# Phase 2 with seven block products instead of eight

## The chip, the cores and the metric

The kernel runs on one core of one Trainium2 chip. The metric is the device time of one execution in microseconds (us). A core has a matmul engine (PE, TensorE; PEld are its weight loads), three engines for elementwise work (DVE, ACT and POOL), and a queue engine (SP) from which this kernel issues its DMAs. Each engine works through its own instructions in the order in which the program puts them; semaphores tie the engines together.

## What is computed

Three layers one after the other, all in float32 (condensed from the reference):

```python
def _attn_ref(q, k, v):                  # 4 batches, 8 heads, 576 positions, 64 wide
    scores = scale * np.matmul(q, k.transpose(0, 1, 3, 2))
    mask = (rel >= 0) & (rel < window)   # causal window of 128, linear bias per head
    attn = softmax(np.where(mask, scores + bias[None], -1000000000.0))
    return np.matmul(attn, v)
def _moe_ref(x, w1, w2, w3, w_out):      # x: 2304 x 512, d_ff 1024
    h = (x @ w1) * (x @ w2) @ w3
    return h @ w_out
def _moe2_ref(x, w_in, w_out):           # d_ff 2048
    h = np.maximum(x @ w_in, 0.0)
    return h * h @ w_out
```

The attention output, 2304 tokens of 512, goes through the first feed-forward layer (called g and y below) and then through the second. Only the second, "phase 2", is computed differently by the change: r = max(x w_in, 0), then o = (r * r) w_out. Weights arrive as 64-bit floats and are made into float32 words on the chip.

## The kernel before

**Precision.** Every float32 operand of a matmul that counts is split into a high part and the rest, each in the format that PE reads at full rate (F32R). A product is then three matmuls, high x high, high x low and low x high, which `mm3` (lines 163 to 166) issues. So each operand costs a copy (the high part) and a subtraction (the low part) on DVE, ACT or POOL before PE can use it.

**Phase 1** holds attention for 32 heads, the first layer's two products and their product (`add_ab`, names `g`, `gf`, `gt`), and the second (`add_y`), which stores y transposed to DRAM, `y_scr`. Its order is made by a planner (`Plan`, lines 28 to 121): each piece of work is a task with a rank, the engines that could do it with an assumed length on each, what it depends on, and the buffers that it takes and gives back. The planner places tasks one by one, the earliest first and the lower rank among those that could start at about the same time, chooses the engine where more than one can do it, and so fixes each engine's order. [...]

**Weights.** A 64-bit word is turned into a float32 word by a scaling (`conv_g`), a shift (`conv_s`) and two shift-and-mask instructions (`conv_m`, line 294) on 1024 columns; `conv_hi` and `conv_lo` split the result. Phase 2's weights are 16 such pieces, `w2io`: piece fi holds 128 columns of w_in and the 128 rows of w_out that belong to them. Six are converted in phase 1 by the planner, ten within the first 512 tokens of phase 2 by a fixed order.

**Phase 2** (`r_step`, `o_step`, lines 934 to 990) is written out by hand. Tokens go in four blocks of 512 and one of 256. For each block and each fi, `r_step` multiplies 128 columns of w_in with the block's y (four inner pieces of 128, three matmuls each, 512 columns wide), ACT takes Relu and Square, and DVE splits the square into `rr`. Two steps later `o_step` multiplies `rr` with the rows of w_out and adds to the block's accumulators in PSUM, one for each 128 tokens (512 columns wide), over all 16 fi. The squares stay in SBUF.

## Time and profile before

| | us |
|---|---|
| median of 3 runs (lowest, highest) | 921.34 (920.14, 923.11) |
| the profiled execution | 921.4 |
| its span, first to last instruction | 919.6 |
| phase 1, to the first r matmul | 515.9 |
| phase 2, first r matmul to the last matmul's end | 399.9 |

The profile's page gives busy times by engine, and a chain that follows the work that ended last back to the start. Rows by line read: line, engine, operation, output<-input by tile names, partitions x elements, how many, then busy time, mean length in nanoseconds, and the idle time before them with what ended it. Rows of stretches read: from:to, length, then the busy time of PE, PEld, DVE, ACT and POOL with counts, the granted clock of PE (1.00 is full), the share of the DMA engines' time and GB/s. Rows of the timeline read: start, length, engine, line, operation; a matmul's length overlaps with the next one's, so the distance between starts is what a matmul costs. POOL's durations are rough.

### The profile page before, as it was taken

To read this page: it belongs to the slowest core of one execution; us is meant where nothing else is said; L and a number is where in the kernel's file an instruction comes from. 1 tells how busy PE (TensorE), PEld (TensorE's weight loads), DVE (VectorE), ACT (ScalarE), POOL (GpSimd) and SP (SyncE) were. 2 spreads that over 40 slices of the span, in tenths; PEclk is the share of its full clock that TensorE was granted. 3 is DMA by queue.
4 is the path that set the end of the run, shared out by engine and by line. 5 is a ranking of instruction groups with operands and counts; after the bars stand their busy time and mean duration, and the time that the engine had idled before them with its cause. 6 is when DMAs were issued, how large, how long until landed. Compare 5 with 4: busy or idle time off the path is not lost.

```text
span 919.6 us, 13785 instructions
## 1 busy us (share of the span) xinstructions
PE 908.6 (99%) x5192; PEld 777.8 (85%) x5192; DVE 515.7 (56%) x1189; ACT 417.5 (45%) x941; POOL 115.7 (13%) x166
## 2 busy tenths in 40 slices
PE   8999999999999999999999999999999999999998
PEld 5544479999999999999999888888888888888897
DVE  5777888787777777786749992132222112221222
ACT  5777776676666666663512442232223222222222
POOL 3323323142312122120000000000000000000000
PEclk9999999999999999999999999999999999999999
DMA  6786321423223132312626430020001000100010
GB/s 234 261 292 196 138 78 33 109 49 83 72 72 85 33 91 66 84 40 70 208 73 229 163 127 12 0 92 1 1 11 69 1 1 12 46 1 1 10 38 24
DMA packets 31075, 73.73 MB, mean 80 GB/s; under 512 B 5793, under 2 KB 14497, under 8 KB 26913
## 3 DMA queue, kind: packets, MB, share of 16 engines
q1 hardware_dynamic: 31008, 72.86, 25.6%
q8 instruction: 41, 0.67, 0.3%
q14 instruction: 26, 0.20, 0.1%
HBM read 63.41 MB, written 9.44 MB: 79 GB/s over the span
## 4 chain that ended last, share of the span: by engine, by line
PE 92%; DVE 4%; issue 1%; DMA 1%; ACT 1%; POOL 0%; SPq 0%; DVEq 0%; POOLq 0%; ACTq 0%
PE g L164 9%; PE g L166 9%; PE g L165 9%; PE o L165 7%; PE o L166 7%; PE o L164 7%; PE r L165 7%; PE r L166 7%; PE r L164 7%; PE g L725 7%; PE s L458 3%; PE t L481 2%; PE a L515 2%; PE s L461 1%; PE s L460 1%; DVE raw L294 1%
## 5 line engine op out<-in xcount | busy, mean ns | idle before, releaser
L947 DVE CAST rr<-s 128x512 fp32r<-128x512 f32 (+1 forms) x80 | 31.9, 399 | 250.0 <-ACT s L946 249.9
L945 ACT ACTIVATE t<-r 128x512 f32<-128x512 f32 (+1 forms) x80 | 44.4, 555 | 264.0 <-PE r L166 264.0
L164 PE MATMUL g<-x,wu 128*128 128x288 f32 x512 | 153.7, 300 | 0.0
L165 PE MATMUL g<-x,wu 128*128 128x288 f32 x512 | 151.5, 296 | 0.0
L166 PE MATMUL g<-x,wu 128*128 128x288 f32 x512 | 151.0, 295 | 0.0
L165 PE MATMUL r<-ys,wu 128*128 128x512 f32 (+1 forms) x320 | 118.8, 371 | 0.0
L166 PE MATMUL r<-ys,wu 128*128 128x512 f32 (+1 forms) x320 | 118.7, 371 | 0.0
L164 PE MATMUL r<-ys,wu 128*128 128x512 f32 (+1 forms) x320 | 118.6, 371 | 0.0
L165 PE MATMUL o<-wu,rr 128*128 128x512 f32 x288 | 113.2, 393 | 0.0
L166 PE MATMUL o<-wu,rr 128*128 128x512 f32 x288 | 112.7, 391 | 0.5 <-DVE rr L172 0.5
L164 PE MATMUL o<-wu,rr 128*128 128x512 f32 x288 | 112.8, 392 | 0.0
L165 PEld LDWEIGHTS g<-x,wu 128*128 128x128 f32 x512 | 96.9, 189 | 0.0
L166 PEld LDWEIGHTS g<-x,wu 128*128 128x128 f32 x512 | 96.5, 189 | 0.0
L164 PEld LDWEIGHTS g<-x,wu 128*128 128x128 f32 x512 | 96.4, 188 | 0.0
L294 DVE SCALAR_TENSOR_TENSOR raw<-raw 128x1024 uint32<-128x1024 uint32 x72 | 91.7, 1277 | 2.3 <-ACT raw L284 1.4
L165 PE MATMUL g<-gt,wu 128*128 128x288 f32 x256 | 75.8, 296 | 0.6 <-DVE gt L172 0.6
L164 PE MATMUL g<-gt,wu 128*128 128x288 f32 x256 | 76.3, 298 | 0.0
L166 PE MATMUL g<-gt,wu 128*128 128x288 f32 x256 | 75.5, 295 | 0.0
L164 PEld LDWEIGHTS r<-ys,wu 128*128 128x128 f32 x320 | 60.2, 188 | 11.7
L165 PEld LDWEIGHTS r<-ys,wu 128*128 128x128 f32 x320 | 60.2, 188 | 11.5
L166 PEld LDWEIGHTS r<-ys,wu 128*128 128x128 f32 x320 | 60.1, 188 | 11.0
L438 ACT ACTIVATE e<-e,st 128x256 f32<-128x256 f32 (+1 forms) x128 | 60.5, 475 | 17.0 <-DVE st L430 16.7
(123 smaller groups left out, 1662.5 us busy)
## 6 DMA issues: line engine op xcount, KB each, us to landing
raw<-in_w2io_dram SPq DMA_DIRECT2D x16, 1024.0 KB, 4.9
qkraw<-in_qk_dram SPq DMA_DIRECT2D x46, 288.0 KB, 4.3
raw<-in_w3t_dram SPq DMA_DIRECT2D x8, 1024.0 KB, 5.5
raw<-in_w_dram SPq DMA_DIRECT2D x8, 1024.0 KB, 5.1
y_scr<-ye SPq DMA_DIRECT2D x32, 144.0 KB, 1.8
out_dram<-ob SPq DMA_DIRECT2D x18, 256.0 KB, 2.4
raw<-in_w_out_dram SPq DMA_DIRECT2D x4, 1024.0 KB, 7.0
yr<-y_scr SPq DMA_DIRECT2D x16, 256.0 KB, 2.7
```

The lines of the kernel that those rows point to most:

```text
L164: nc.tensor.matmul(o, wh, xh, start=start, stop=False)
L165: nc.tensor.matmul(o, wh, xl, start=False, stop=False)
L166: nc.tensor.matmul(o, wl, xh, start=False, stop=stop)
L294: nc.vector.scalar_tensor_tensor(out=low, in0=high, scalar=(3, 0x80000000)[part], in1=low, op0=(ALU.logical_shift_left, ALU.bitwise_and)[p ...
L438: nc.scalar.activation(out=e, in_=e, func=ACTF.Exp, bias=st[:, 0, i:i + 1], scale=-1.0, accum_out=st[:, 1, i:i + 1],)
L458: nc.tensor.matmul(o, qb, d["kh"][:, k0:k1], start=True, stop=True)
L460: nc.tensor.matmul(o, qb, d["kh"][:, k0:k1], start=True, stop=False)
L481: nc.tensor.transpose(t[:, 128 * c:128 * c + 128], src, ident)
L515: nc.tensor.matmul(a[:, 128 * kb:128 * kb + w], vs[:, kb, :], pt[:, 0, c:c + w], start=kb == 0, stop=kb == 2,)
L725: nc.tensor.matmul(gw[fi], wl, wr, start=c == 0, stop=c == 7)
L945: nc.scalar.activation(out=t, in_=o, func=ACTF.Relu)
L947: nc.vector.tensor_copy(out=rr[:, 0, 0:n], in_=s)
```

## The change

Both products of phase 2 are computed by Strassen's scheme in Winograd's form: the matrices are cut into 2 x 2 blocks, sums of blocks are formed first, seven block products are taken instead of eight, and further sums give the four blocks of the result.

**r.** The three token ranges of 768 are passes j = 0, 1, 2. In a pass, w_in's 2048 columns are cut into halves (a row of the one belongs to one of the other 1024 away; m counts 8 pieces of 128 in a half), the inner 512 into halves of 256 and the tokens into halves of 384. A group (j, m) has seven products P1 to P7 into PSUM banks `X` (five), each of two inner pieces x three matmuls of 384 columns (`p_r`). Then `add_group` forms the sums: c1 (a copy of P1, on ACT), U2, U3 and U4 and the four results `C` (four buffers), seven DVE instructions that read PSUM. ACT takes Relu and Square of each C, and it is stored to DRAM, `s_scr`. All of r is done before o begins.

**o.** Nine groups t of 256 tokens. The squares are read back (four tiles of 128 partitions x 8 x 128, in runs of 512 bytes), four combinations of 1024 columns are formed (`fc0` to `fc3`), seven operands are split (`oh`, `ol`, 1024 columns, tiles `ww` and `st`), and each of the seven products has 8 inner pieces x three matmuls of 256 columns (`p_o`). Sums as above, then stores to the output.

**Weights.** All 16 conversions are now planner tasks of rank 500 and up behind the first layer's weights, inside phase 1; the words go to DRAM (`m_scr`). Piece m is read back when it is needed, combined (four sums of 256 columns, `cb`) and split into seven blocks: tile `u` for four of them (1024 columns) and `v6` or `u` for three (768). The ten `u` and six `v6` tiles hold all of w_in's blocks until the last pass of r lets go of them one after the other, and only then take w_out's.

**Order.** Phase 2 is in the planner now, with PE's products in a fixed sequence and all other work placed around them. Tile pools are opened at the points where the memory of the stage before is free: `fo` after pass 1 of r, `fq` and `ww` after the last product of r and the last o weights.

The diff, cut to its core:

```diff
+    TN = 384
+    NJ = NT // (2 * TN)
+    NM = NF2 // 2
+    s_scr = [dram.tile([NF2, 128, 2 * TN], F32, name=f"s_scr{j}") for j in range(NJ)]
+    m_scr = {(k, m): dram.tile([128, 1024], F32, name=f"m_scr{k}{m}") for k in "io" for m in range(NM)}
-            pt1=1, pt2=1, a=1, b=1, xf=1, ta=1, tb=1, g=3, asb=2, gf=2, gt=8, ye=2, w2v=4, yr=2,
+            pt1=1, pt2=1, a=1, b=1, xf=1, ta=1, tb=1, g=3, asb=2, gf=2, gt=8, ye=2,
+            yA=14, yB=6, s0=1, t2a=1, t2b=1, v6=6, st=2, c1=2, U2=1, U4=1, U3=1, C=4, X=5, fo=4, fq=5, ww=4,
...
-    def r_step(j, fi):
-        n = blocks[j][1]
...
-        for k in range(K1):
-            mm3(o, w[:, 0, k * 128:(k + 1) * 128], w[:, 1, k * 128:(k + 1) * 128],
-                y[:, 0, k, 0:n], y[:, 1, k, 0:n], k == 0, k == K1 - 1)
...
-        nc.scalar.activation(out=t, in_=o, func=ACTF.Relu)
-        nc.scalar.activation(out=s, in_=t, func=ACTF.Square)
-        nc.vector.tensor_copy(out=rr[:, 0, 0:n], in_=s)
-        sub(nc.vector, rr[:, 1, 0:n], s, f(rr[:, 0, 0:n]))
-        rt[j, fi] = rr
...
-        for i in range(nt):
-            mm3(acc[j][i], rr[:, 0, i * 128:(i + 1) * 128], rr[:, 1, i * 128:(i + 1) * 128],
-                w[:, 0], w[:, 1], fi == 0, fi == NF2 - 1)
-    LAG = 2
-    steps = [(j, fi) for j in range(NB) for fi in range(NF2)]
...
+    A_AT = {1: "a0", 2: "a1", 3: "b2", 4: "a3", 5: "b0", 6: "b1", 7: "a2"}
+    B_AT = {1: "a0", 2: "a2", 3: "a3", 4: "b2", 5: "b0", 6: "b1", 7: "a1"}
+    PO = (1, 6, 7, 5, 2, 3, 4)
+    ORDER = ((1, 2, 4, 6, 7, 5, 3), PO)
...
+    def open_q1():
+        att.close()
+        psb.close()
+        q = q1.enter_context(tc.tile_pool(name="q1", bufs=1, side="right", reuse_waits="tile"))
+        pool.update(yA=q, s0=q, t2a=q)
+        ps = late.enter_context(tc.tile_pool(name="ps_x", bufs=1, space=PSUM, reuse_waits="tile"))
+        pool.update(X=ps)
...
+    def open_fo():
+        yst.close()
+        pool["fo"] = yst.enter_context(tc.tile_pool(name="fo", bufs=1, reuse_waits="tile"))
+
+    def open_q2():
+        q1.close()
+        q = q1.enter_context(tc.tile_pool(name="q2", bufs=1, side="right", reuse_waits="tile"))
+        pool.update(fq=q, ww=q)
...
+    def m_last(k, m):
+
+        r = raws[k, m]
+        nc.vector.scalar_tensor_tensor(
+            out=flat(r), in0=r[:, :, 1], scalar=0x80000000, in1=r[:, :, 0],
+            op0=ALU.bitwise_and, op1=ALU.bitwise_or,
+        )
+
+    def m_store(k, m):
+        nc.sync.dma_start(out=m_scr[k, m], in_=f(flat(raws.pop((k, m)))))
...
+    def combine(kind, i, M, S, e):
+
+        if kind == "A":
+            o, a, op, b = (
+                (S(0), M(2), ALU.add, M(3)), (S(1), S(0), ALU.subtract, M(0)),
+                (M(2), M(0), ALU.subtract, M(2)), (S(2), M(1), ALU.subtract, S(1)),
+            )[i]
+        else:
+            o, a, op, b = (
+                (S(0), M(1), ALU.subtract, M(0)), (S(1), M(3), ALU.subtract, S(0)),
+                (M(1), M(3), ALU.subtract, M(1)), (S(2), M(2), ALU.subtract, S(1)),
+            )[i]
+        ENG[e].tensor_tensor(out=o, in0=a, in1=b, op=op)
...
+        add("ms" + z, rank, {"dma": w_dma(524)}, lambda e: m_store(k, m), ["cn" + z], [], ["raw" + z])
+
+    def add_words2(k, m, rank, stag, dep=()):
...
+        add("mb" + z, rank - 3, {"dma": w_dma(524)}, lambda e: m_back(k, m, stag), ["ms" + z, *dep], ["st" + z])
+        src, gm, gs = ["mb" + z], ["st" + z], ["st" + z]
...
+        n = NJ if k == "i" else NT // 256
+        for part, w, tag in (("a", 1024, "u"), ("b", 768, "u" if m < 2 else "v6")):
+            hold(f"w{part}{z}", tag, n * (4 if part == "a" else 3))
...
+            add(f"wh{part}{z}", rank + 0.1, w_copy(w), hi, d, [f"w{part}{z}"], g_)
+            add(f"wl{part}{z}", rank + 0.1, w_tt(w), lo, [f"wh{part}{z}"], [], g_)
...
+        where = ["yA"] * 14 if j != 1 else ["yB"] * 6 + ["yA"] * 8
...
+    def p_r(j, m, P):
+        o = p_bank(("r", j, m), P, TN)
+        wh, wl = w_of("i", m, P)
+        for c in range(2):
+            y = yo[j, P, c]
+            mm3(o, wh[:, 128 * c:128 * c + 128], wl[:, 128 * c:128 * c + 128], y[:, 0], y[:, 1], c == 0, c == 1)
+
+    def p_o(t, P):
+        o = p_bank(("o", t), P, 256)
+        a = ow.pop((t, P))
+        for c in range(NM):
+            bh, bl = w_of("o", c, P)
+            mm3(o, a[:, 0, 128 * c:128 * c + 128], a[:, 1, 128 * c:128 * c + 128], bh, bl, c == 0, c == NM - 1)
...
+        for i, P in enumerate(order):
+            deps, gives, fn = prod(P)
+            hold(f"X{P}{z}", "X", 2 if P == 7 else 1)
+            add(f"P{P}{z}", rank + i, {"pe": w}, fn, deps + [x for x in lastp if x], [f"X{P}{z}"], gives)
+            lastp[0] = f"P{P}{z}"
...
+        add("c1" + z, -20, w_copy(n, True), lambda e: copy(e, t_("c1", "c1"), bank[g, 1]), ["P1" + z], ["c1" + z], [f"X1{z}"])
+
+        def plus(nm, o, tag, P, i, deps, ho, gives):
+            def fn(e):
+                nc.vector.tensor_tensor(out=t_(o, tag), in0=bank[g, P], in1=cs[g, i], op=ALU.add)
+
+            add(nm + z, -20, w_tt(n, "d"), fn, [f"P{P}{z}"] + [x + z for x in deps], [ho + z], [f"X{P}{z}"] + [x + z for x in gives])
+
+        plus("u2", "U2", "U2", 6, "c1", ["c1"], "U2", ["c1"])
+        plus("u3", "U3", "U3", 7, "U2", ["u2"], "U3", ["U2"])
+        plus("u4", "U4", "U4", 5, "U2", ["u2"], "U4", ["U2"])
+        plus("c22", "22", "C", 7, "U4", ["u4"], "C22", ["U4"])
+        plus("c11", "11", "C", 2, "c1", ["c1"], "C11", ["c1"])
+        plus("c12", "12", "C", 3, "U4", ["u4"], "C12", ["U4"])
+        plus("c21", "21", "C", 4, "U3", ["u3"], "C21", ["U3"])
...
+                    nc.scalar.activation(out=x, in_=x, func=ACTF.Relu)
+                    nc.scalar.activation(out=x, in_=x, func=ACTF.Square)
...
+            for c in ("11", "12", "21", "22"):
+                add(f"sq{c}{z}", rank + 16, {"a": 2 * w_copy(TN)["a"]}, lambda e, c=c: sq(e, c), [f"c{c}{z}"])
+                add(f"ss{c}{z}", -15, {"dma": w_dma(197)}, lambda e, c=c: st(c), [f"sq{c}{z}"], [], [f"C{c}{z}"])
...
+            def ld(e, k=k, i=i, h=h):
+                x = fa[t, k] = new(ft[k], [128, NM, 128])
+                nc.sync.dma_start(
+                    out=x, in_=s_scr[j][NM * h:NM * h + NM, :, t0 + 128 * i:t0 + 128 * i + 128].rearrange("c p t -> p c t")
+                )
...
+        add(f"fc0{t}", rank, w_tt(1024), lambda e: comb(0, e), [f"lfA21{t}", f"lfA22{t}", "q2"], F("S1"), F("A21", "A22"))
+        add(f"fc1{t}", rank, w_tt(1024), lambda e: comb(1, e), [f"lfA11{t}", f"fc0{t}"], F("S2"), F("S1", "A11"))
+        add(f"fc2{t}", rank + 3, w_tt(1024), lambda e: comb(2, e), [f"fc0{t}", f"lfA11{t}"], [], F("A11", "A21"))
+        add(f"fc3{t}", rank + 5, w_tt(1024), lambda e: comb(3, e), [f"fc1{t}", f"lfA12{t}", f"ol6{t}"], [], F("A12", "S2"))
+        src = {1: f"lfA11{t}", 6: f"fc1{t}", 2: f"lfA12{t}", 7: f"fc2{t}", 5: f"fc0{t}", 3: f"fc3{t}", 4: f"lfA22{t}"}
+        order = ORDER[t > 0]
+        chain = {}
...
+            tag = "st" if P in (1, 2) else "ww"
+            hold(f"ow{P}{t}", tag, 1)
...
+    add("fo", 0, {"gate": 0.0}, lambda e: open_fo(), [f"P{P}r1{NM - 1}" for P in range(1, 8)])
+    add("q2", 0, {"gate": 0.0}, lambda e: open_q2(), last_r + [f"wlao{NM - 1}", f"wlbo{NM - 1}"])
+
+    prev = [f"clw12{i}" for i in range(8)]
+    for x, (k, m) in enumerate([(k, m) for k in "io" for m in range(NM)]):
+        add_merge(k, m, 500 + x, prev)
+        prev = [f"ld{k}{m}"]
...
+    prev = done(2)
+    for m in range(NM):
+        add_words2("o", m, 2090 + 7 * m, "st" if m < NM - 1 else "s0", prev)
+        prev = [f"mbo{m}"]
+    for t in range(NT // 256):
+        add_o(t, r, False)
+        r += 7
```

Where instructions now stand, at three places. First PE, phase 2. Before, the products of r and o alternate; `r` and `o` are their PSUM tiles, `ys` and `rr` the moving operands and `wu` the weights:

```order
L166 MATMUL r<-ys,wu 128x512
L164 MATMUL o_6146<-wu,rr 128x512
L165 MATMUL o_6146<-wu,rr 128x512
L166 MATMUL o_6146<-wu,rr 128x512
L164 MATMUL o_6147<-wu,rr 128x512
```

Now, at the one place where r ends and o begins (`yA`: y's split blocks, `st`: the first o operand):

```order
L166 MATMUL X<-yA,u 128x384
L167 MATMUL X<-yA,u 128x384
L168 MATMUL X<-yA,u 128x384
L166 MATMUL X<-u,st 128x256
L167 MATMUL X<-u,st 128x256
L168 MATMUL X<-u,st 128x256
```

All r matmuls stand ahead of all o matmuls, the former 384 and the latter 256 columns wide.

DVE at the same place of the changed kernel. Rows of line 1089 are sums that read `X`; line 174 is the subtraction of a split, and line 1160 a combination of o's operands:

```order
L1089 TENSOR_TENSOR C_8335<-X_8314,U4_8311 128x384
L1089 TENSOR_TENSOR C_8338<-X_8326,U3_8293 128x384
L174 TENSOR_TENSOR u_8306<-st_8193,u_8306 128x1024
L174 TENSOR_TENSOR v6_8308<-st_8193,v6_8308 128x768
L174 TENSOR_TENSOR u_8345<-s0_8235,u_8345 128x1024
L174 TENSOR_TENSOR v6_8349<-s0_8235,v6_8349 128x768
L174 TENSOR_TENSOR st_8352<-fo_7627,st_8352 128x1024
L1160 TENSOR_TENSOR fq_8364<-fo_7795,fo_7823 128x1024
L1160 TENSOR_TENSOR fq_8393<-fq_8364,fo_7627 128x1024
L174 TENSOR_TENSOR st_8355<-fo_7653,st_8355 128x1024
```

The second row is the last sum of r. Behind it stand the splits of o's weight rows 6 and 7, then the first product's operand (`st_8352`), two combinations, and the second product's operand (`st_8355`).

ACT between pass 0 and pass 1 of r. Lines 1115 and 1116 are Relu and Square, line 171 is a copy; `yB` and `yA` are the next pass's operands:

```order
L171 ACTIVATE yA_6920<-st_6831 128x384
L1115 ACTIVATE C_6827<-C_6827 128x384
L1116 ACTIVATE C_6827<-C_6827 128x384
L1115 ACTIVATE C_6899<-C_6899 128x384
L1116 ACTIVATE C_6899<-C_6899 128x384
L171 ACTIVATE c1_6949<-X_6927 128x384
L1115 ACTIVATE C_6915<-C_6915 128x384
L1116 ACTIVATE C_6915<-C_6915 128x384
L171 ACTIVATE yB_6957<-st_6831 128x384
```

`c1_6949` copies the first product of the new pass; `yB_6957`, an operand of its third product, stands behind it and behind one more pair of squares.

More of the change, by code (lines that the diff above doesn't have):

```diff
@@ L866, in fused_kernel @@
-    p2 = ExitStack()
-    def open_w2():
-        att.close()
-        w2_pool[0] = p2.enter_context(
-            tc.tile_pool(name="w2", bufs=1, side="right", reuse_waits="tile")
-        )
-        ys[0] = w2_pool[0].tile([128, 2, K1, 512], F32R, tag="ys", bufs=1, name="ys")
-    def t_yr(k):
-        t = yr[0, k] = w2_pool[0].tile([128, 512], F32, tag="yr", bufs=2, name="yr")
-        nc.sync.dma_start(out=t, in_=y_scr[k, :, 0:512])
-    def t_ysh(k, e):
-        copy(e, ys[0][:, 0, k], yr[0, k])
@@ new lines, in open_ph @@
+    def open_ph():
+        p1.close()
+        q = late.enter_context(tc.tile_pool(name="ph", bufs=1, reuse_waits="tile"))
+        pool.update({k: q for k in ("v6", "st", "t2b", "c1", "U2", "U3", "U4", "C")})
+        pool["yB"] = yst.enter_context(tc.tile_pool(name="yb", bufs=1, reuse_waits="tile"))
+    def open_fo():
[5 more added lines that the diff above has]
+        pool.update(fq=q, ww=q)
@@ new lines, in new, with m_load @@
+    def new(tag, shape, dt=F32):
+        n = plan.caps[tag]
+        return (wp if tag == "u" else pool[tag]).tile(shape, dt, tag=tag, bufs=n, name=tag)
+    mw = {}
+    sw = {}
+    wq = {}
+    mst = {}
+    def m_load(k, m):
+        t = raws[k, m] = new("u", [128, 1024, 2], U32)
+        o = 0 if k == "i" else 1024
+        for h in range(2):
+            nc.sync.dma_start(
+                out=t[:, 512 * h:512 * h + 512, :].rearrange("p n w -> p (n w)"),
+                in_=w2io[m + NM * h].bitcast(U32)[:, o:o + 1024],
+            )
```

291 lines of the change are left out of this document (202 added, 89 removed).

## The prediction

> **What bounds the kernel now.** I read the page's busy times and its chain of waits first, then PE's waits, then the stretch in which phase 2 runs.
>
> ```profile
> span 919.6 us, 13785 instructions
> PE 908.6 (99%) x5192; PEld 777.8 (85%) x5192; DVE 515.7 (56%) x1189; ACT 417.5 (45%) x941; POOL 115.7 (13%) x166
> PE 92%; DVE 4%; issue 1%; DMA 1%; ACT 1%; POOL 0%; SPq 0%; DVEq 0%; POOLq 0%; ACTq 0%
> PE o L166 <- DVE rr L172: 0.5, 1, 0.5
> ```
>
> PE is busy for 99% of the span, the chain that ended last lies on PE for 92% of it, and in phase 2 PE waited once, for 0.5 us. So phase 2 costs what its matmuls cost, and fewer matmul columns shorten it, as long as the other engines still keep up. The next two fences, the timeline and the groups by line, give counts and spacing.
>
> ```profile
> 515.89 0.40 PE L164 MATMUL r<-ys,wu 128*128 128x512 f32 x1
> ...
> 865.07 0.28 PE L164 MATMUL r<-ys,wu 128*128 128x256 f32 x1
> ...
> 866.38 0.28 PE L166 MATMUL r<-ys,wu 128*128 128x256 f32 x1
> ...
> 915.44 0.39 PE L166 MATMUL o<-wu,rr 128*128 128x512 f32 x1
> ```
>
> ```profile
> L165 PE MATMUL o<-wu,rr 128*128 128x512 f32 x288 | 113.2, 393 | 0.0
> L165 PE MATMUL r<-ys,wu 128*128 128x512 f32 x256 | 100.8, 394 | 0.0
> L165 PE MATMUL r<-ys,wu 128*128 128x256 f32 x64 | 18.0, 282 | 0.0
> ```
>
> Each row is one of three lines, so phase 2 has 3 x (288 + 256) = 1632 matmuls of 512 columns and 192 of 256. It lasts from 515.89 to 915.44 + 0.39, 399.9 us. A mean duration (393 ns) overlaps with the next matmul; what counts is the distance of starts. Twelve matmuls of 256 columns start within 1.31 us, 0.119 each. The 512-column ones then have (399.9 - 192 x 0.119 - 0.5) / 1632 = 0.231 (0.5 is the one wait).
>
> **The matmuls.** r becomes 3 x 8 groups of 7 products of 6 matmuls, 1008 of 384 columns. At the middle between 0.119 and 0.231, 0.175, they take 176.4 us. o becomes 9 groups of 7 products of 24, 1512 of 256 columns; at 0.119 they take 179.9. Together 356.3, so **-43.6 us**. The 0.119 was only seen in runs of twelve between wider matmuls. The nearest long run is that of the 288-column ones (73 starts, 0.132 each):
>
> ```profile
> 506.24 0.29 PE L166 MATMUL g<-gt,wu 128*128 128x288 f32 x1
> ...
> 515.76 0.29 PE L166 MATMUL g<-gt,wu 128*128 128x288 f32 x1
> ```
>
> So o lies between 179.9 and 1512 x 0.132 = 199.6; I take the lower end, since 0.119 and 0.132 stand in the ratio that their columns and a small constant give.
>
> **What each group now asks of the other engines.** Durations from the groups by line:
>
> ```profile
> L172 DVE TENSOR_TENSOR wu<-raw,wu 128x1024 fp32r<-128x1024 f32 x24 | 29.6, 1235 | 1.8 <-ACT wu L169 1.2
> L172 DVE TENSOR_TENSOR pt<-t,pt 128x512 fp32r<-128x512 f32 x50 | 34.3, 685 | 10.5 <-ACT pt L169 10.3
> L778 DVE TENSOR_TENSOR gf<-g,a_sb 128x288 f32<-128x288 f32 x64 | 29.2, 456 | 31.1 <-PE g L166 29.0 <-ACT e L209 1.0 <-PE s L460 0.4
> L169 ACT ACTIVATE wu<-raw 128x1024 fp32r<-128x1024 f32 x18 | 20.9, 1162 | 21.0 <-DVE raw L294 17.6 <-issue 2.7 <-DVE wu L172 0.8
> L213 DVE CAST wu<-raw 128x1024 fp32r<-128x1024 f32 x6 | 4.2, 693 | 0.2
> L946 ACT ACTIVATE s<-t 128x512 f32<-128x512 f32 x64 | 40.4, 632 | 2.1 <-DVE rr L172 0.4
> L946 ACT ACTIVATE s<-t 128x256 f32<-128x256 f32 x16 | 6.7, 417 | 0.5
> L169 ACT ACTIVATE a_sb<-g 128x288 f32<-128x288 f32 x64 | 26.2, 409 | 57.2 <-PE g L166 55.9 <-PE s L460 1.1
> L172 POOL TENSOR_TENSOR x<-xf,x 128x288 fp32r<-128x288 f32 x5 | 4.2, 859 | 23.4 <-ACT x L169 16.4 <-DVE x L213 7.0
> ```
>
> A sum out of PSUM at 384 columns lies between 456 (288) and 685 (512): 0.55 us; at 256, 0.42. An r group has 7 such sums on DVE, 3.9 us, and on ACT the copy c1 (about 0.49, from 409 at 288) and 8 Relu/Square of 0.525 (middle of 417 and 632), together 4.7. PE needs 42 x 0.175 = 7.35. In 13 of the 24 groups (six in the first pass, seven in the third) a weight row is prepared too: two copies on ACT (1.16 and, scaled to 768 columns, 0.9), two subtractions on DVE (1.235 and 0.95), four sums of 256 mostly on POOL (about 0.8 each). That makes ACT 6.8, DVE 6.1 and POOL 3.2 of 7.35: still cover, but thin. Five PSUM banks and four C tiles must carry every late hand-over. Bounds: nothing, and 13 x 1 us; I take **+3**.
>
> An o group has on DVE 4 combinations and 7 subtractions of 1.235, 7 sums of 0.42 and about two of its seven copies (0.693): 17.9 us against PE's 7 x 24 x 0.119 = 20.0. A DVE full of work loses little:
>
> ```profile
> 490.00:524.50 34.50, 33.91 (x227) 31.81 (x225) 33.33 (x46) 12.34 (x20) 0.00 (x0) 1.00 0.54 188
> ```
>
> Third of the busy times is DVE's, 33.33 of 34.5, 97%. 17.9 / 0.97 = 18.5 stays under 20.0; it starts with no lead, so **+1** (0 to 10).
>
> **The seam between r and o.** Nothing of o but the halves of its first two operands can be ready before r ends: the last weight tile of o needs the slot that the last r product frees, and all eight rows of o weights are needed by the first o product. DVE's rows in the front part stand in this order after the last r sum: `u` 1024, `v6` 768, `u` 1024, `v6` 768, `st` 1024. So from the last r matmul's end PE waits for the sum (0.55) and 3 x 1.235 + 2 x 0.95, with about 0.4 for hand-overs: **+6.6 us**. ACT's copies (1.16 and 0.9, then `st` 1.16) run beside and end sooner. Cover for this would be a free weight slot, and there is none. The second o product's operand `st` stands behind two combinations on DVE, 3 x 1.235 = 3.7 us against the first product's 2.86: **+0.9**. From the third on DVE is ahead.
>
> A PE that has stood still also starts more slowly here. The timeline at the kernel's begin shows the same transposes twice:
>
> ```profile
> 17.25 0.42 PE L490 MATMUL t<-ident,p 128*128 128x128 f32 x1
> 17.46 0.42 PE L491 MATMUL t<-ident,e 128*128 128x128 f32 x1
> ...
> 26.55 0.27 PE L490 MATMUL t<-ident,p 128*128 128x128 f32 x1
> 26.66 0.27 PE L491 MATMUL t<-ident,e 128*128 128x128 f32 x1
> ```
>
> Starts are 0.21 apart at first and 0.11 later, half the rate. No row shows a gap of several us later on, so the cost after 6.6 us of waiting lies between 0 and one o product at double spacing, 2.9; I take **+1.4**. [...]
>
> **Between passes of r.** Pass 1, the second, needs 14 new operand tiles, a copy and a subtraction each; eight of them get their slots only as pass 0's last group frees them. ACT's rows hold ten of the tile copies (about 0.5 each) beside the squares in the last group of pass 0, and three in the first group of pass 1: 7.8 and then 9.4 us of ACT against 7.35. The third product of pass 1 needs a copy (`yB`) that stands behind a c1 copy, which waits for the first product of that pass, and a square; added up along ACT's rows it starts about 2.2 us late, and two later ones 0.3 each: **+2.8** (0 to 5). Pass 2 begins with six tiles prepared ahead: nothing.
>
> **Phase 1.** All 16 conversions now run there, where six did: 20 more shifts and masks of 1024, and on the other side fewer weight splits.
>
> ```profile
> L294 DVE SCALAR_TENSOR_TENSOR raw<-raw 128x1024 uint32<-128x1024 uint32 x72 | 91.7, 1277 | 2.3 <-ACT raw L284 1.4
> 200.00:300.00 100.00, 100.00 (x779) 99.55 (x778) 75.16 (x221) 64.62 (x174) 25.62 (x36) 1.00 0.29 72
> ```
>
> That is 20 x 1.277 = 25.5 us more on DVE, about 35 with the first operands of r. In 200 to 300 DVE is idle for a quarter and PE for nothing; eight conversions (8 x 2.55 us and some of their scalings) stand among heads 13 to 31, a stretch of some 240 us, and raise DVE to about 86%. The other eight stand behind attention. The order of PE keeps 660 first-layer matmuls behind the last attention output where 636 stood, so the reserve that hides a late head stays. **+1.5** (-1 to 8); without that cover, rival 3.
>
> **The end.** The last sum is 0.42 and its store 128 KB, where a copy of 0.69 and 256 KB stood:
>
> ```profile
> yr<-y_scr SPq DMA_DIRECT2D x16, 256.0 KB, 2.7
> yr<-y_scr SPq DMA_DIRECT2D x4, 128.0 KB, 2.0
> ```
>
> About **-0.6** at most; I take -0.4. The sum goes against the profiled execution's own 921.4 us, 0.06 above the median of the runs: 921.4 - 43.6 + 3 + 1 + 6.6 + 0.9 + 1.4 + 2.8 + 1.5 - 0.4 = **894.6**, forecast **894.5**.
>
> **The rivals.** (1) *ACT and the C tiles pace r.* A square stands in line, its store lands over 2 us later, and only then is the tile free for the next group's sum, which holds a bank. For it: ACT at 6.8 of 7.35. Against it: 24 groups have four tiles each for 7.35 us, nearly twice what sum, square and store add up to (0.55 + 1.05 + about 2.35, between the two transfers above). With 8.4 us per prepared group: 13 x 1.05 = 14 more, 908. [...]
>
> (2) *The loads of o pace it; slower than before.* Each o group loads four tiles of 1024 runs of 512 bytes, 64 runs per DMA engine. Price of a run:
>
> ```profile
> q1 hardware_dynamic: 31008, 72.86, 25.6%
> 9.00:11.00 2.00, 2.00 (x6) 1.00 0.99 406
> ```
>
> A packet took 0.256 x 919.6 x 16 / 31008 = 121 ns at 2350 bytes. At the best rate seen, 406 GB/s over 16 engines, the bytes alone are 93, so 28 is fixed and 512 bytes would take 48: 12 us per group, hidden in 20.0. If a short run costs as much as a mean one, it is 31 us per group, and the o phase grows by 9 x 11 = 99: 993. It decides from 78 ns; from 90 on the kernel is slower than before.
>
> (3) *Attention falls behind.* If half of DVE's 35 us in phase 1 is paid by PE: 894.5 + 17 = 911. Against: DVE's idle quarter.
>
> (4) *256 columns do not hold 0.119.* At 0.132, 19.7 more: 914. That is also what remains if the change saves far fewer columns in time than in number.
>
> **How the numbers follow.** Forecast 0.66 (885 to 905), rival 1 0.13, rival 2 0.07, rival 3 0.06, rival 4 0.04; 0.04 for what I have not seen, mostly slower. The low end, 885, is the sum with the seam's smaller terms and r's waits gone (about 9.5 less); the high end, 912, holds rival 1 and most of rival 3. A measurement tells 0.3% (2.8 us) from no change. Faster: 0.66 + 0.13 + 0.05 + 0.04 = 0.88 less a little for rivals that go further, 0.87; same 0.03; slower 0.10.
>
> **What would show it.** PE's starts at 0.175 and 0.119; one wait of 6 to 7 us for a DVE `st` subtraction before the first o product, and one near 2 us for a `yA` tile about 58 us into phase 2; first r matmul near 517. Wrong would be: hundreds of short waits of PE on sums in r (rival 1), DVE waiting for `fq` or `fo` loads (2), a first r matmul after 525 (3), o matmuls further than 0.125 apart (4).

## The result, and the profile after

The changed kernel takes 899.36 us (median of four runs, 898.94 to 901.4); before, in the same set of runs, 920.74 (919.34 to 923.11). The ratio is 0.977, with a 95% interval from 0.9744 to 0.9795: **faster by 2.3%, 21.4 us of the 26.8 that the sum had**. The prediction of 894.5 is 4.9 us too low; the time lies in its range.

The page after, its busy times and the shares of its chain by engine:

```profile
span 899.6 us, 16224 instructions
PE 871.2 (97%) x5888; PEld 805.3 (90%) x5888; DVE 696.4 (77%) x1402; ACT 502.4 (56%) x1086; POOL 205.6 (23%) x252
PE 80%; DMA 9%; DVE 7%; ACT 2%; issue 2%; SPq 1%; POOL 0%; DVEq 0%; ACTq 0%; POOLq 0%
PE X L168 13%; PE X L167 13%; PE X L166 13%; PE g L166 7%; PE g L168 7%; PE g L167 7%; PE g L730 7%; DMA u<-in_w2io_dram 3%; DMA m_scro<-u 2%; PE s L463 2%; PE a L520 2%; PE s L466 1%; PE t L486 1%; PE s L465 1%; DMA m_scri<-u 1%
```

PE still bounds the kernel, but the chain has 9% on DMAs, and 6% of these are the loads and stores by which phase 2's weights are converted. The profiled execution took 901.4 us. Timeline of PE at the points that cut it into stages (start, length, engine, line, operation; in brackets the idle time and who ended it):

```profile
526.51 0.34 PE L166 MATMUL X<-yA,u 128*128 128x384 f32 x1
...
527.93 0.34 PE L168 MATMUL X<-yA,u 128*128 128x384 f32 x1
...
709.53 0.34 PE L168 MATMUL X<-yA,u 128*128 128x384 f32 x1
713.25 0.38 PE L166 MATMUL X<-u,st 128*128 128x256 f32 x1 [3.38 <-ACT st L171]
713.47 0.28 PE L167 MATMUL X<-u,st 128*128 128x256 f32 x1
715.71 0.58 PE L168 MATMUL X<-u,st 128*128 128x256 f32 x1 [1.96 <-DVE st L174]
...
721.17 0.28 PE L166 MATMUL X<-u,st 128*128 128x256 f32 x1
...
896.32 0.28 PE L168 MATMUL X<-v,ww 128*128 128x256 f32 x1
```

The first r matmul starts at 526.51 where it was 515.89: phase 1 has become 10.6 us longer. Phase 2 then takes 370.1 us (to 896.32 + 0.28) where it took 399.9, 29.8 less. Eight steps of r from 526.51 to 527.93 are 1.42 us, 0.1775 each; the 1484 steps of o from 721.17 to 896.32 are 0.118 each, small waits included. All of PE's waits in phase 2:

```profile
PE X L166 <- ACT st L171: 3.4, 1, 3.4
PE X L167 <- DVE yB L174: 2.3, 3, 1.0
PE X L168 <- DVE st L174: 2.0, 1, 2.0
PE X L168 <- DVE u L174: 1.6, 2, 1.3
```

That is seven waits (columns: us in all, times, longest): two at the seam between r and o, three at the boundary between pass 0 and pass 1 of r, two for weight tiles in pass 0. Of phase 1, PE's waits before, ...

```profile
PE t L614 <- POOL bm L196: 3.4, 1, 3.4
PE t L489 <- DVE pt L172: 1.3, 1, 1.3
```

... and after:

```profile
PE t L619 <- POOL bm L204: 3.4, 1, 3.4
PE t L486 <- POOL e L213: 2.7, 3, 1.2
PE g L166 <- DVE gf L783: 2.0, 4, 1.1
PE g L168 <- DVE wu L174: 1.7, 1, 1.7
```

After has 21 waits spread over attention and the first layer, 15.3 us in all with the smaller ones, where before had six waits and 6.5 us; the 3.4 us at the start are in both. They are the symptom; the experiments look for what is behind them.

### The profile page after: what moved, and what is told of

The parts are those of the page before. It is cut to its first block, busy times and chain, and to the rows that moved or that the text cites. A ratio compares the mean times of both kernels' runs of the same rounds, so it can differ in the third digit from the quotient of the medians.

```text
span 899.6 us, 16224 instructions
## 1 busy us (share of the span) xinstructions
PE 871.2 (97%) x5888; PEld 805.3 (90%) x5888; DVE 696.4 (77%) x1402; ACT 502.4 (56%) x1086; POOL 205.6 (23%) x252
## 4 chain that ended last, share of the span: by engine, by line
PE 80%; DMA 9%; DVE 7%; ACT 2%; issue 2%; SPq 1%; POOL 0%; DVEq 0%; ACTq 0%; POOLq 0%
PE X L168 13%; PE X L167 13%; PE X L166 13%; PE g L166 7%; PE g L168 7%; PE g L167 7%; PE g L730 7%; DMA u<-in_w2io_dram 3%; DMA m_scro<-u 2%; PE s L463 2%; PE a L520 2%; PE s L466 1%; PE t L486 1%; PE s L465 1%; DMA m_scri<-u 1%
## 5 line engine op out<-in xcount | busy, mean ns | idle before, releaser
L167 PE MATMUL g<-gt,wu 128*128 128x288 f32 x256 | 75.8, 296 | 0.1
L1089 DVE TENSOR_TENSOR C<-X,U 128x384 f32<-128x384 f32 (+1 forms) x99 | 51.0, 518 | 24.4 <-PE X L168 11.1
L1115 ACT ACTIVATE C<-C 128x384 f32<-128x384 f32 x96 | 49.5, 515 | 32.6 <-DVE C L1089 32.5
L168 PE MATMUL X<-yA,u 128*128 128x384 f32 x192 | 65.2, 340 | 1.6 <-DVE u L174 1.6
L167 PE MATMUL X<-yA,u 128*128 128x384 f32 x192 | 65.0, 339 | 0.0
L166 PE MATMUL X<-yA,u 128*128 128x384 f32 x192 | 65.0, 339 | 0.0
L938 POOL TENSOR_TENSOR st<-st 128x256 f32<-128x256 f32 (+1 forms) x52 | 46.7, 916 | 76.4 <-DMA st<-m_scri 37.1
L730 PE MATMUL g<-raw 128*128 128x512 f32 x128 | 63.2, 625 | 0.0
L213 POOL TENSOR_SCALAR e<-e,st 128x256 f32<-128x256 f32 (+1 forms) x61 | 31.0, 520 | 122.1 <-DVE st L453 73.0
L167 PE MATMUL X<-u,ww 128*128 128x256 f32 x198 | 55.4, 280 | 0.0
L168 PE MATMUL X<-u,ww 128*128 128x256 f32 x198 | 55.4, 280 | 0.0
L166 PE MATMUL X<-u,ww 128*128 128x256 f32 x198 | 55.4, 280 | 0.0
L171 ACT ACTIVATE pt<-t 128x512 fp32r<-128x512 f32 (+1 forms) x64 | 38.2, 597 | 28.0 <-PE t L498 18.5
```

The costliest lines, as they stand in the source:

```text
L166: nc.tensor.matmul(o, wh, xh, start=start, stop=False)
L167: nc.tensor.matmul(o, wh, xl, start=False, stop=False)
L168: nc.tensor.matmul(o, wl, xh, start=False, stop=stop)
L171: nc.scalar.activation(out=o, in_=i, func=ACTF.Copy)
L213: nc.gpsimd.tensor_scalar(out=o, in0=i, scalar1=c, scalar2=1.0, op0=ALU.mult, op1=ALU.mult)
L730: nc.tensor.matmul(gw[fi], wl, wr, start=c == 0, stop=c == 7)
```

## The experiments on phase 1

Each kernel ran beside the kernel before. "First r" is the start of the first r matmul in the one profiled execution of each; 515.9 before, 526.5 after.

| kernel | median, us (range) | ratio to before (95%) | first r |
|---|---|---|---|
| the change | 899.36 (898.94-901.4) | 0.977 (0.9744-0.9795) | 526.5 |
| no conversions at all | 893.27 (892.66-894.24) | 0.9703 (0.9686-0.9719) | 516.1 |
| conversion instructions left out, loads and stores kept | 900.47 (895.44-902.96) | 0.9771 (0.9738-0.9803) | 526.8 |
| planner frees the tile later (2.4 us) | 890.8 (890.2-893.29) | 0.9678 (0.9661-0.9694) | 517.0 |
| the same, once more | 889.88 (889.07-892.38) | 0.967 (0.9654-0.9686) | 516.2 |
| no conversion instructions, the change's own order of DMAs | 899.34 (896.3-903.59) | 0.9774 (0.9735-0.9812) | 525.3 |
| that, loads don't wait for stores | 892.21 (890.66-894.91) | 0.97 (0.9675-0.9726) | 517.2 |
| planner frees the tile 4.8 us later, first o operand early | 889.61 (889.34-890.74) | 0.9669 (0.9654-0.9684) | 516.1 |

The kernels at 900.47 and 899.34 scatter by more than 7 us between executions, the others by 1 to 5.

How a piece is converted matters here. It takes one of two spare `u` tiles, its words come by two DMAs (`m_load`), four instructions work on them, and `m_store` writes the result to DRAM; only when that store has landed can the next piece's load use the tile. All of these DMAs are issued by SP, in one line with attention's loads and y's stores. The DMAs of after between 200 and 500, with KB each and median us to landing:

```profile
u<-in_w2io_dram SPq DMA_DIRECT2D x28, 512.0 KB, 4.3
m_scri<-u SPq DMA_DIRECT2D x8, 512.0 KB, 2.8
m_scro<-u SPq DMA_DIRECT2D x8, 512.0 KB, 4.4
```

The explanations at the start: the order puts work where its words have not landed yet, the instructions themselves take too much of DVE and ACT, or the traffic holds up attention's own loads.

**No conversions.** `add_merge` is not called, and y's words stand in for phase 2's weights (its products are other numbers, of the same size and count).

```diff
-        add_merge(k, m, 500 + x, prev)
-        prev = [f"ld{k}{m}"]
+        pass
...
-        nc.sync.dma_start(out=t[:, 0:1024], in_=m_scr[k, m])
+        nc.sync.dma_start(out=t[:, 0:1024], in_=y_scr[m % 4, :, 0:1024])
```

> Left out: everything that phase 1 does for phase 2's weights (16 loads, conversions and stores); where a weight row is read back later, words of y are read instead, so the output is not the reference's. All theories of the late first r matmul (526.5 us against 515.9) put its cause here, so all expect it at 516 (514 to 519) and a time of about 890. If it stays at 524 or later, the cause is elsewhere: in the first operands of r, or in the order of attention.

The first r matmul came at 516.1. So the whole price of phase 1, 10.4 of 10.6 us, hangs on the conversions. (r itself took 185.6 us here against 183.0: its waits fell differently, and matmuls at half rate, 0.32 us apart instead of 0.18, followed them up to 588.4; that is why the time is not lower still.)

**Loads and stores alone.** The four instructions are taken out of the plan; the piece is loaded and its raw words stored. y's words stand in for the weights again.

```diff
-        add("cg" + z, rank, w_ts(1024), lambda e: conv_g((k, m), e), ["ld" + z])
-        add("cs" + z, rank, w_ts(1024, "Da"), lambda e: conv_s((k, m), e), ["ld" + z])
-        add("cm" + z, rank, {"D": 1.23}, lambda e: conv_m((k, m), e, 0), ["cg" + z, "cs" + z])
-        add("cn" + z, rank, {"D": 1.23}, lambda e: m_last(k, m), ["cm" + z])
-        add("ms" + z, rank, {"dma": w_dma(524)}, lambda e: m_store(k, m), ["cn" + z], [], ["raw" + z])
+        add("ms" + z, rank, {"dma": w_dma(524)}, lambda e: m_store(k, m), ["ld" + z], [], ["raw" + z])
```

> Left out: the four conversion instructions of each of the 16 weight rows; their loads and stores stay, and words of y stand in for the weights as in the run without anything. Theory A (conversion instructions stand at the head of an engine's line before their words have landed) and theory B (the conversions are simply too much work for DVE): first r matmul at 516 to 518, as with nothing at all. Theory C (32 loads and 16 stores of half a megabyte slow down attention's own loads): still 523 to 527.

Nothing was gained, 526.8, though no instruction was left to compete for DVE. But the kernel had changed more than meant: without the instructions to space them, the loads of 15 of the 16 pieces now went out between 164 and 275 us, where they had reached to 477. The stretch from 200 to 300 after, and here (busy PE, PEld, DVE, ACT, POOL, clock, DMA share, GB/s):

```profile
200.00:300.00 100.00, 97.41 (x745) 95.57 (x744) 81.81 (x231) 65.52 (x175) 27.08 (x40) 1.00 0.40 115
```

```profile
200.00:300.00 100.00, 93.60 (x690) 91.34 (x689) 68.34 (x205) 57.99 (x163) 23.35 (x28) 0.97 0.79 238
```

With the DMA share at 0.79 instead of 0.40 this run says that the DMAs alone can cost it, not that they did in the change. It was repeated in a better form below.

**The tile counted as taken until its store has landed.** One line of the planner: a tile whose last user is one of these stores is free 2.4 us after the planner thought. No work is taken away and none added; only the order changes.

```diff
-                last[h] = max(last[h], fin)
+                last[h] = max(last[h], fin + (2.4 if n.startswith("ms") else 0.0))
```

> All work kept; in the planner's account alone a conversion's tile comes free 2.4 us later than its store's end there, about when the store lands in the trace (4.4 us for 512 KB against 1.95 in the account). Theory A: conversions are put into the engines' orders later, fewer of them stand waiting for a load, DVE's idle time before the scalings of these words falls from 16.7 us to under 8, and the first r matmul moves from 526.5 to 519 to 522; total 893 to 897. Theories B and C: the same work and the same traffic, 525 to 528 and no change of the total.

890.8 us, first r at 517.0: 9.5 of the 10.6 us are gone, with all conversions in place. (So phase 1 costs 1.1 us more than before, 0.3 in the repeat further down; the prediction gave the work 1.5.) Who waited longest for the loaded words (52 us in all), after:

```profile
  ACT u L294: 26.3, 7
  DVE u L215: 16.7, 7
```

and with the line changed (17 us in all):

```profile
  POOL u L213: 7.5, 5
  DVE u L215: 4.3, 2
```

On these rows I took the mechanism to be this: DVE and ACT stand at a conversion whose words are not there, with attention's and the first layer's instructions behind it, as in this piece of DVE's timeline after, where a `gf` that PE is waiting for comes right behind a wait of 3.32 us:

```profile
454.42 0.70 DVE L215 TENSOR_SCALAR u<-u 128x1024 f32<-128x1024 f32 x1 [3.32 <-DMA u<-in_w2io_dram]
455.03 0.45 DVE L783 TENSOR_TENSOR gf<-g,a_sb 128x288 f32<-128x288 f32 x1
```

But the line moves the loads in SP's queue as well as the conversions on the engines, so this run alone can't tell. The next one takes the engines out.

**The same DMAs at the same places, no instructions.** The planner keeps the time of the four instructions, so SP's order is that of the change; they are just not issued. y's words stand in for the weights.

```diff
-        add("cg" + z, rank, w_ts(1024), lambda e: conv_g((k, m), e), ["ld" + z])
+        add("cg" + z, rank, w_ts(1024), lambda e: None, ["ld" + z])
```

(likewise `cs`, `cm` and `cn`.)

> The change with the same loads and stores of phase 2's weight words at the same places in the queue's order as in the change itself (the planner still counts the conversions' time), but with the four conversion instructions of each piece not issued, so that y's words stand in for phase 2's weights and the output is another. If engines that stand behind words not yet landed cost the 10 us: nobody waits for these loads, PE loses nothing in phase 1, first r matmul at 516 to 518, time 889 to 892. If the traffic itself costs it (attention's own loads come later beside it): first r matmul at 522 to 527, with PE or DVE waits that lead to qkraw or vraw loads, time 895 to 900. The earlier run without these instructions had all loads at once between 200 and 300, which this one doesn't.

899.34 us, first r at 525.3. **Engines in line behind unlanded words are not the only way to the loss**: no engine waits for these words here, and nearly the whole loss remains. But neither do the waits lead to late attention loads, as the rival had it: from 150 us to r, DVE and ACT waited 16 us for `qkraw` before and 14 here. What both kernels have is SP standing still. SP's own waits from 150 to 527 after ...

```profile
SPq L902 <- DMA m_scro<-u: 23.4, 6, 5.7
SPq L902 <- DMA m_scri<-u: 21.5, 8, 4.5
```

... and here:

```profile
SPq L902 <- DMA m_scri<-u: 28.8, 7, 6.0
SPq L902 <- DMA m_scro<-u: 26.4, 5, 6.4
```

SP comes to a load (L902) whose tile is not free, and stands there until the store from that tile has landed: 45 us in 14 stops after, 55 in 12 here, and 8 and 10 more where the first tiles of y take their turn. (In the run with loads and stores alone SP stood at the other end, 41 us before stores whose load had not landed.) Behind it stand the loads of attention, y's stores and the loads of y. Rows of SP's timeline in this kernel show it at a load of y's first tiles (L987), which wait for the same stores: from 476.98, when the store is issued, SP issues nothing for 6.1 us, and the two y stores that go out at 483.90 and 484.84 have stood behind it.

```profile
476.55 0.43 SPq L919 DMA_DIRECT2D m_scro<-u  x1
483.06 0.79 SPq L987 DMA_DIRECT2D u<-y_scr  x2
483.90 0.42 SPq L831 DMA_DIRECT2D y_scr<-ye  x1
...
484.84 0.46 SPq L831 DMA_DIRECT2D y_scr<-ye  x1
```

ACT needs a `ye` tile back (`ACT ye L171 <- DMA y_scr<-ye`, one wait of 5.0 us between 440 and 500), and PE needs the bank that ACT empties:

```profile
489.14 0.40 PE L166 MATMUL g<-x,wu 128*128 128x288 f32 x1 [3.15 <-ACT ye L171]
```

**The same, but no load waits for a store.** The store copies the input's words from DRAM to DRAM instead of from the tile. Bytes and places in the queue stay; only the waits for these stores, at L902 and at L987, lose their reason. (SP still stood 14.9 us in 4 stops at L902, for the load that was last in the tile.) The weights are y's words still.

```diff
-        nc.sync.dma_start(out=m_scr[k, m].bitcast(U32), in_=flat(raws.pop((k, m))))
+        raws.pop((k, m))
+        nc.sync.dma_start(out=m_scr[k, m].bitcast(U32), in_=w2io[m].bitcast(U32)[:, 0:1024])
```

> The kernel before it (no conversion instructions, y's words as phase 2's weights) with one thing changed: the words that go to DRAM are copied there from the input in DRAM and not from the tile, so the bytes loaded and written are the same and at the same places in the queue, but a load no longer waits on SP until the store from its tile has landed. If SP, which stands at such a load with attention's loads and y's stores behind it, costs the 10 us (65 us of SP's waits there were for these stores): first r matmul at 516 to 518, time 889 to 892. If the traffic costs it: first r matmul at 522 to 527, time 895 to 900.

892.21 us, first r at 517.2. The stretch from 400 to 500, first with the wait and then without it:

```profile
400.00:500.00 100.00, 96.24 (x728) 95.39 (x727) 46.10 (x118) 33.94 (x85) 8.95 (x11) 1.00 0.61 192
```

```profile
400.00:500.00 100.00, 100.00 (x762) 99.90 (x761) 51.19 (x121) 33.56 (x83) 9.52 (x11) 1.00 0.58 186
```

PE gets 34 more matmuls into the same 100 us, at nearly the same traffic. So with the instructions gone it is not the traffic either: **SP, standing at a load for a tile whose store has not landed, is what the two kernels differ in**, and their medians are 7.1 us apart with ranges that don't meet. Not all of it can be followed. PE's rows of the two profiled executions, laid side by side, come apart by 1.4 us before the first of these loads (issued at 146.24 and 144.87), by 2.1 from there to 300, most of it a stretch at half rate behind a wait that both have (1.65 and 1.47 us; granted clock 0.93 and 1.00 between 225 and 250), and by 4.5 between 486 and 497, at the wait shown above and in the matmuls behind it. These 4.5 us are traced to SP.

The planner let SP stand there because it gave the tile back at the store's issue plus 1.95 us where landing takes 2.8 to 4.4. In the change itself the same order also reaches PE through the engines. Between 440 and 500 ACT stood 23.5 us there before loaded words; PE waited four times for a `gf` (2.0 us), as in the rows at 454, and once for a `ye` (0.5); and between 450 and 500 it got 338 matmuls done, against 380 in both executions with the planner's line. So the late load is common to both kernels, while the path from it to PE differs. How much of the change's loss took each path, the runs don't divide.

Nor are the microseconds that SP stands a price. SP's waits for these stores in the same stretch with the planner's line, where 9.5 of the 10.6 us are gone:

```profile
SPq L902 <- DMA m_scri<-u: 14.4, 6, 3.5
SPq L902 <- DMA m_scro<-u: 10.7, 4, 3.6
```

That is 25 us in 10 stops where the change had 45 in 14. What counts is presumably what stands behind a stop and how soon it is needed; no run varied that alone.

**4.8 us instead of 2.4.** With the edit to the first o operand that is described below.

> Both edits that gave the shortest time so far (tile counted as taken after its store's issue, first o operand early) with 4.8 us in the planner's account in place of 2.4. If SP's waits for the stores of these tiles are what is left (26 us of them with 2.4), they go to under 8 us, the loads move later in the queue, the first r matmul comes at 516 and the time is within 1 us of the 888.4 of both edits, at best 0.5 less. Rival: 2.4 was right by luck and any other order of the same tasks scatters by several us: first r matmul between 516 and 522 in no relation to SP's waits.

The first r matmul came at 516.1, and SP's waits at L902 for these stores fell to 3.1 us, as the theory had it. (SP now stood 75.8 us at the stores instead, until the words were converted, where the change had 19.4, and phase 1 was no longer for it.) The time did not follow: 889.61. Later loads made the first weight tiles and y operands of r late (PE waited 1.8 us for ACT's `u`, 2.0 for DVE's `u`, 2.0 for a `yB`), and r took 186.2 us instead of 182.5. Here 2.4 did as well.

## The experiments on the seam and on the loads of o

Four kernels with the planner's line in them (first r near 517), run together, and the earlier one without it:

| kernel | median, us (range) | ratio to before (95%) | last r to last o matmul |
|---|---|---|---|
| the change, first o operand early | 898.75 (898.32-901.95) | 0.9766 (0.9747-0.9786) | 183.4 (186.8 in the change) |
| planner's line alone | 889.88 (889.07-892.38) | 0.967 (0.9654-0.9686) | 186.9 |
| with a filler on PE | 890.13 (887.91-893.0) | 0.9669 (0.9648-0.9689) | 185.9 |
| with the first o operand early | 888.38 (886.52-891.43) | 0.9652 (0.9632-0.9672) | 183.4 |
| with short runs in o's loads | 891.57 (889.32-892.72) | 0.9681 (0.9663-0.9698) | 187.1 |

**First o operand early.** In the change the two `st` operands of the first o group wait for the last but one weight row; here the first asks only for the row ahead of that, and its subtraction goes first among what is ready.

```diff
-(["wlao6", "wlbo6"] if t == 0 and tag == "st" else [])
+(["wlao6", "wlbo6"] if t == 0 and P == 2 else ["wlao5", "wlbo5", "mbo6"] if t == 0 and P == 1 else [])
...
-            add(f"ol{P}{t}", rank + pos, w_tt(1024), lo, [f"oh{P}{t}"], [], F(k))
+            add(f"ol{P}{t}", 0 if t == 0 and P == 1 else rank + pos, w_tt(1024), lo, [f"oh{P}{t}"], [], F(k))
```

On the change itself:

> Only the seam between r and o is changed: the first o product's operand is copied and split as soon as a tile is free, ahead of the last two weight rows, not behind them. My account of the seam (DVE's line of splits sets it; the first product's matmuls for the first six weight rows need only their own operand): PE waits about 2 us for the sum and one split, runs the first product in between the rest, waits again 1 to 2 us, never long enough to lose its clock, and the second product ends about 3.5 us earlier (2.5 to 4.5) after the last r matmul than in the changed kernel (13.9 us). Rival: the eight weight rows are needed before any o matmul; then nothing changes, 0 to 0.5 us.

On top of the planner's line:

> The base, and the first o operand is prepared ahead of the last weight row of o. Theory: the wait ahead of o goes from 3.4 + 2.0 us to about 1.6, 0.5 and 1.3 us spread over three products as in the earlier run with this edit, PE is never idle long enough for the half rate, and the o phase from last r to last o matmul shortens by 3.5 us: about 887.3. Rival, what was gained there is paid back by r, whose last pass then shares ACT and DVE with these tasks (r was 1.9 longer in the earlier run): about 889 to 891.

The repeat of the base beside it:

> The change with the planner counting a conversion's tile as taken until 2.4 us after its store was issued, once more, as the base of the three kernels beside it. All theories: 890.8 again within 1 us, first r matmul at 517, last r matmul to first o matmul 3.7 us, last o minus last r matmul about 185.7.

Both times the way from the last r to the last o matmul is 183.35 us, as it is with 4.8 us in the planner. Without this edit it measures 185.7 to 187.1 in nine profiled executions, 185.7 and 186.9 in the two of the same kernel with the planner's line: the waits are alike (3.38 us, then 1.67 or 1.96; with the filler, further down, 0.36, then 1.96), and the half rate behind them, starts 0.21 apart instead of 0.12, lasts 2.3 to 5.7 us. So 2.3 to 3.8 us are gained; the 3.5 of the expectations is the gain against a slow one. PE's waits there are now spread (two of the four with the planner's line):

```profile
700.25 0.39 PE L168 MATMUL X<-u,st 128*128 128x256 f32 x1 [1.61 <-DVE st L174]
...
705.39 0.39 PE L168 MATMUL X<-u,st 128*128 128x256 f32 x1 [1.26 <-DVE st L174]
```

No half-rate matmuls follow: one step of 0.22 behind each wait, then 0.12 again. In the whole time less of it shows: 0.6 us on the change, where r itself took 1.9 us longer (184.9; ten half-rate matmuls between its passes are 1.4 of that), and 1.5 with the planner's line, inside the scatter of both. 888.38 is the shortest time measured, 3.5% below the kernel before; that it beats 889.88 is not shown.

**A filler.** Seven float32 matmuls that nobody reads stand on PE behind the last r product (14 records in the profile, two for each; 3.19 us in all, 0.46 for one, where a matmul of the split operands, F32R, takes 0.12 at the same width).

```diff
...
+        for _ in range(7):
+            nc.tensor.matmul(t[:, 0:256], ident, bm, start=True, stop=True)
...
```

> The base plus seven matmuls of 256 columns in plain float32 right behind the last r product, which nobody reads, on PE while it waits for the first o operand. Theory: the half-rate matmuls from 706 to 711 come from the idle stretch ahead of them; with PE busy in it the first o product runs at 0.118 spacing at once and PEclk stays 1.00, 2.2 us less; but its end now comes before the second operand is ready, so PE waits about 0.9 us there, and the time is 1.3 us below the base. Rival, half rate belongs to the first matmuls of a new kind of product (first use of these weight tiles) and not to idleness: spacing 0.213 stays, time within 0.3 us of the base.

The timeline at the seam:

```profile
699.34 3.19 PE L1266 MATMUL g<-bm,ident 128*128 128x256 f32 x14
702.88 0.38 PE L166 MATMUL X<-u,st 128*128 128x256 f32 x1 [0.36 <-ACT st L171]
...
705.35 0.58 PE L168 MATMUL X<-u,st 128*128 128x256 f32 x1 [1.96 <-DVE st L174]
...
708.50 0.36 PE L167 MATMUL X<-u,st 128*128 128x256 f32 x1
```

The filler covered the first wait, and the first o matmul started 0.36 us after it; but after the second wait, 1.96 us, the half rate came all the same, starts 0.21 apart from 705.73 to 708.50 and 0.12 behind that. The time did not move (+0.3), and a half rate of 3 us lies within what the same seam shows without a filler. Neither theory had it: the half rate came here without the first wait (0.36 us instead of 3.38), and it is not the new weight tiles either, since with the first operand early the same tiles start at full rate (0.12).

**Short runs.** Each tile of o is read back by two DMAs in runs of 256 bytes.

```diff
...
+                for q_ in range(2):
+                    a_ = t0 + 128 * i + 64 * q_
+                    nc.sync.dma_start(
+                        out=x[:, :, 64 * q_:64 * q_ + 64], in_=s_scr[j][NM * h:NM * h + NM, :, a_:a_ + 64].rearrange("c p t -> p c t")
+                    )
```

> The base, and each tile that o reads back comes by two DMAs in runs of 256 bytes instead of one in runs of 512, so 512 runs per DMA engine and group instead of 256, with the same bytes. In the stretch from 740 to 820 of the change a packet took 0.528 x 80 x 16 / 22062 = 31 ns at 549 bytes, 8 us of 19.7 per group. Theory, a run costs what its bytes cost: still 8 to 10 us, hidden, within 1 us of the base. Rival, a run has a fixed price of some 31 ns: 512 x 31 = 16 us per group plus the stores, DMA share near 0.9, operands late now and then, 0 to 10 us slower. Second rival, a short run costs twice as much as one of 512: 32 us per group against 19.7, o longer by 9 x 12 = 100 us.

DMA queues between 740 and 820 with the planner's line alone, and with short runs (packets, MB, share):

```profile
q1 hardware_dynamic: 21062, 11.56, 50.2%
```

```profile
q1 hardware_dynamic: 36968, 10.84, 60.6%
```

A packet took 0.502 x 80 x 16 / 21062 = 30.5 ns at 549 bytes, and 0.606 x 1280 / 36968 = 21.0 at 293. A line through these two points, an estimate, gives a run some 10 ns and 0.037 ns a byte. With 75% more packets the share rises by a fifth, PE had no wait for these loads, and the way through o is the same (187.1 against 186.9).

## Why the prediction was right, and where it was not

| term of the sum | predicted | in the profile after |
|---|---|---|
| matmuls, with o's +1 | -42.6 | -42.6 |
| waits inside r's passes | +3 | +1.4 |
| boundary of pass 0 and 1 | +2.8 | +2.9 |
| waits at the seam, two operands | +7.5 | +5.7 |
| slow start at the seam | +1.4 | +2.5 |
| phase 1 | +1.5 | **+10.6** |
| end | -0.4 | -0.8 |

How the right column comes out: 1008 x 0.1775 + 1512 x 0.118 = 357.3 against 399.9. r lasts 709.53 - 526.51 + 0.18 = 183.2, of which matmuls 178.9 and the three `yB` gaps 2.9 (starts 0.78, 1.27 and 1.35 apart, less 0.18 each); 1.4 remain. At the seam 713.25 - 709.53 - 0.18 and 715.71 - 713.47 - 0.12 make 5.7; the 25 steps from there to 721.17 took 5.5 instead of 3.0. The right column adds up to -20.3, the profiled execution lost 20.0. That the time lies in the range owes something to luck: phase 1 was 9.1 us above its term, and the other terms together came out 2.6 below theirs. (The range is given as 885 to 905, and its high end worked out as 912; the time lies in both.)

**Matmuls, right.** 0.175 and 0.119 were read between rows of 288, 512 and twelve of 256 columns; 0.1775 and 0.118 came, one a little more and one a little less. Rival 4 (0.132) is out.

**r and its passes, right.** Rival 1, ACT and the C tiles, didn't come: no wait of PE for a bank and two for weight tiles. The boundary came out in size and not in shape: three waits for `yB`, 0.6, 1.1 and 1.2 us, where the working had 2.2 and twice 0.3, and the last paragraph a `yA` tile. The sum out of PSUM took 554 ns at 384 columns and 421 at 256 (forecast 0.55 and 0.42).

**The seam, right in size, not in its cut.** The prediction had one wait before the first o product, for the low half. PE in fact starts two matmuls on the high half after 3.4 us and then waits 2.0 for the low one; the second product, for which it had 0.9 us of waiting, never waits, because the first runs at half rate (25 steps in 5.5 us instead of 3.0) and lasts longer. The smaller waits and the larger slow start nearly cancel: 8.2 of 8.9. The slow start is no fixed size: by the ways measured above it cost 1.4 to 2.9 us in nine executions, with waits alike. The 1.4 that was taken lies at the low end of this range, the 2.5 of the change's profiled execution within it.

**Loads of o, right.** 30.5 ns per packet where rival 2 needed 78 to decide. The lower figure that the prediction worked out, 48 ns for 512 bytes, was still too high, since it put 28 ns on each run where the line through the two points above gives 10.

**Phase 1, the step that failed.** The prediction counted 25.5 and then 35 us more on DVE, set it against DVE's idle quarter, and took +1.5 with 8 as the bound. As a price of the work this was right: 0.3 and 1.1 us with the planner's line. As a forecast it failed: the first r matmul came at 526.5, past the 525 that the prediction had named as the sign of rival 3. What it left out is in SP's rows, not in DVE's. It counted the conversions as instructions and not as DMAs: 32 loads and 16 stores of 512 KB in the one queue that feeds attention, where 16 loads of 1 MB had stood, 13 of them before r and 12 of these from 433 us on, and no store; and two tiles through which all of it goes round. It had the order of the change to read, and quoted no row of SP. The page before already showed transfers of 256 KB that take 2.7 us to land, while the planner gives the tile of a 512 KB store back after 1.95; that SP would stop at nearly every load (14 of 16 pieces) could be worked out from this and the two tiles, though not what a stop costs. Rival 3 gave 17 us for attention falling behind, if half of DVE's new work was paid by PE. Where it can be followed, between 440 and 500, it was the first layer's `gf` and `ye` that came late, and not for the amount of work: words came late and SP stood.

## What to carry to other kernels

In this kernel's one queue, a DMA that had to wait for a buffer held up everything behind it: in the change 14 stops of up to 5.7 us at the loads of phase 2's weights. When work moves to another stage, count its DMAs in that queue and ask of each what its buffer waits for and how long that takes to land; the idle quarter of DVE said nothing on it. If an order is planned ahead, a buffer that a store reads is free when the store has landed (2.8 and 4.4 us after the issue here, by the medians, where the account had 1.95), and the account must say so; here that one line was worth 9 us, nearly half as much as the whole change. And before a wait is called the cause, take it away alone: here the most visible waits, those of DVE and ACT for loaded words, could be removed with hardly any gain, since the late load reached PE another way.

## What the runs showed of the hardware that was not expected

**Half rate after short waits, and not every time.** At the boundary of pass 0 and 1, PE's three waits are alike in two executions of one and the same kernel, the one with the planner's line (starts 0.78, 1.28 and 1.37 apart, and 0.79, 1.28 and 1.35; matmuls of 384 columns at 0.18 between them). In the first these rows follow:

```profile
582.74 0.69 PE L167 MATMUL X<-yB,u 128*128 128x384 f32 x1 [1.03 <-DVE yB L174]
583.22 0.52 PE L168 MATMUL X<-yB,u 128*128 128x384 f32 x1
...
585.46 0.51 PE L166 MATMUL X<-yA,u 128*128 128x384 f32 x1
```

Seven steps in 2.24 us, 0.32 each. In the second the full rate goes on:

```profile
581.94 0.44 PE L167 MATMUL X<-yB,u 128*128 128x384 f32 x1 [1.02 <-DVE yB L174]
582.22 0.34 PE L168 MATMUL X<-yB,u 128*128 128x384 f32 x1
```

Of ten profiled executions with three such waits here, six have the half rate behind them and four, the change's among them, don't. (In the other two changed kernels the waits fell otherwise.) With the filler it was there, and the granted clock in that stretch was 0.55:

```profile
582.00:585.50 3.50, 3.44 (x11) 3.44 (x12) 2.56 (x7) 1.66 (x4) 1.01 (x1) 0.55 0.31 112
```

So waits of 0.45 to 1.08 us, three within 6 us, had the half rate behind them (0.32 a step instead of 0.18) in six executions, and in four the same waits had not. What decides between the two, no run shows.
